# Scores of the second queries of batch 0 from 64-row tiles, and a hand-set order from the first instruction

## Chip, cores and metric

The kernel runs on one core of one Trainium2 chip. The metric is the device time of one execution in microseconds (us). The kernel before took 816.43 us, the median of three runs (814.87 to 817.64).

## The reference

Block-causal attention feeds a gated convolution network, all in float32:

```python
scores = q @ k.T / sqrt(64)                       # 8 batches, 8 heads, 576 tokens, 64 wide
scores = where(query block >= key block, scores, -1e9)       # blocks of 64 tokens
x = concat over heads of softmax(scores) @ v      # 8 x 576 x 512
h = relu(x @ w_in)                                # w_in 512 x 1024
gate = sigmoid(conv3(h, conv_w))                  # along tokens, one filter per column
out = (h * gate) @ w_out                          # w_out 1024 x 512
```

The three weights come as float64 and are decoded on the chip.

## The kernel before, in words

**Precision.** Matmuls take float32r operands. Each operand is held as a rounded part and a remainder (`qh`/`ql`, `kh`/`kl`, `wih`/`wil`), and a product is the sum of three matmuls: high by high, low by high, high by low.

**Visits.** The work is cut into visits, each for a pair of heads. Batch 0 gets four visits "A" (queries 0 to 255), then four visits "B" (queries 256 to 575). The other seven batches get 28 whole visits. During the A visits the weights `w_in` are loaded and decoded, during the B visits `w_out`. The feed-forward matmuls (`ffn`, L1142 and L1201) of a batch are spread over the visits that follow it.

**A visit.** Queries and keys are transposed on TensorE (`first_t` L741 for A, `stage_t` L671 for the others), and ScalarE and VectorE evict the high and low parts. For an A visit the two heads of a pair lie in partitions 0-63 and 64-127 of `qa`, `qb`, `kh`, `kl`, and `stage_sa` (L881) multiplies them there: matmuls of 64 rows, head 0 and head 1 by turns, into two PSUM banks (L894). For a B or whole visit, `stage_t` issues DMAs on SyncE's queue that build stacked operands of 128 rows: `qa`/`qb` (high over low of one head, L730), `ka`/`kb` (the high keys twice, L730), and `qz` (a head's high part with zeros in the other half, L708). `stage_s` (L765) then needs two matmuls of 128 rows per block of 128 queries and head: L815 (`ka`,`qa`) and L817 (`kl`,`qz`). In B visits a third one adds the mask (L811). Then come a maximum on VectorE (L825), exp with sums on ScalarE (L828), sum and reciprocal on VectorE (L779, L784) and a scaling on GpSimd (L790). The last 64 queries of both heads share a block of their own (L856). After that the probabilities are transposed (L975), split again (L985 to L994) and multiplied by the values (L1066).

**Order.** Every operation is an `Op` with a target time. `Plan.order` (L97) places all of them with a table of costs and writes out one fixed order for each engine. Where it expects TensorE to stand idle for more than `LEAST`, it inserts dummy matmuls (`work`, L1324, called fills here). They write a score bank that is about to be used, and do nothing else. Targets come from the constants at L264 to L303. Each engine works through its own list strictly in order. In the kernel before, `manual_schedule` is entered only for that list (L1329). What stands ahead of it (identities, mask tile, memsets of kept tiles, L331 to L365) is placed by the framework.

**Counters.** A DMA's end is signalled by one of eight counters, DMAHW0 to DMAHW7. They are dealt out by turns in the order in which the DMAs are recorded. A DMA that gets a counter which an earlier DMA holds is issued only after that one has landed. This wait stands in the queue of the engine that issues it.

**The start.** `load_first` (L431) loads queries, keys and values of batch 0 into `ptbh` and `ptbl`. The keys of pair 0 are issued from ScalarE's queue (L442), all else from SyncE's. The first real work is the transposes of pair 0 (L749).

Of the kernel before, what the change touches and what calls it, by code (L numbers as in the profile page):

```python
# [9 lines left out]
F32 = mybir.dt.float32  # L10
F32R = mybir.dt.float32r
# [222 lines left out]
def kernel(  # L234
# [29 lines left out]
    SLOT, SLOTA, SLOTB = 10.93, 3.2, 5.63  # L264
    WOFF, WSTEP, WLEAD = 1.32, 4.64, 8.03
    WOFF2, WSTEP2 = 38.12, 4.08
    OXA, OPVA, OTA = 3.27, 4.0, 0.13
    OXB, OPVB, OTB = 4.44, 11.35, 4.4
    OX, OPV, OT = 6.73, 18.46, 10.65
    VLEAD, NLEAD, NB, CONV = 2.32, 3.83, 7.53, -0.16  # L270
    OFA, OFB, OF, OXS = 3.54, 7.96, 1.07, 2.1
    FA, FB = 57.6, 86.67
# [3 lines left out]
    JS0, JS1, JS2, JS3, JS4, JS5, JS6, JS7 = -0.1, 0.0, 0.0, 0.0, 1.2, 0.0, 0.06, 0.0  # L276
    JX0, JX1, JX2, JX3, JX4, JX5, JX6, JX7 = 0.14, 0.64, 0.61, 0.25, 0.0, 0.0, 0.0, 1.14
    JP0, JP1, JP2, JP3, JP4, JP5, JP6, JP7 = 0.0, 0.51, 0.28, 1.31, 0.0, 0.67, -0.11, 0.07
    JT1, JT2, JT3, JT4, JT5, JT6, JT7, JT8 = 0.0, 0.0, 0.01, 0.2, -0.38, 0.64, 0.0, 0.0
    JW0, JW1, JW2, JW3, JW4, JW5, JW6, JW7 = 0.64, 2.05, -0.14, 0.0, 1.79, 0.0, 0.74, 1.76  # L280
    JW8, JW9, JWA, JWB, JWC, JWD, JWE, JWF = 0.12, 1.04, 0.06, -0.23, 0.0, -0.41, 0.0, 0.0
    JD0, JD1, JD2, JD3, JD4, JD5, JD6, JD7 = -2.82, 0.0, -1.25, 0.74, 2.2, -0.87, -1.36, 0.0
    JL8, JL9, JLA, JLB, JLC, JLD, JLE, JLF = 0.12, -0.07, 0.0, 0.0, -0.08, 0.0, -1.04, 0.41
# [5 lines left out]
    SKIP = 5.33  # L289
    LEAST, SPARE = 0.42, 0.11  # L290
# [6 lines left out]
    PMASK = ("B",)  # L297
# [3 lines left out]
    LQ, LQS, LV, LVS = -60.0, 7.42, -56.75, 4.18  # L301
    WL0, WLS = -55.92, 2.96
    WINDOW = 20.06  # L303
# [51 lines left out]

    ident = cp.tile([P, P], F32, tag="ident", name="ident")
# [195 lines left out]
    def split(f, parts, src, hi, lo, scratch, deps, bufs, at, go):  # L552
# [39 lines left out]
        o1 = pl.op(ACT, c_act(512), fh, at + 1, deps=[x[0] for x in o], bufs=bufs)  # L592
        o2 = pl.op(PE, c_mm(512), less, at + 1, deps=[o1], bufs=[fb])
        o2 = pl.op(PE, c_mm(512), rest, at + 1, deps=[o2] + [x[1] for x in o], bufs=bufs + [fb])
        wdone[f] = pl.op(DVE, c_dve(512, two_in=True) - 0.03, fl2, at + 1, deps=[o2], bufs=bufs + [fb])
# [168 lines left out]

    def stage_s(ops, hh, at, part, shared):  # L765
# [5 lines left out]
        st = keep([P, 16], F32, "st", 2, EPS)  # L771
        pb, done, exps = {}, {}, {}

        def finish(blocks, st, c0, t0):
            a, b_, w_ = c0 + blocks[0], c0 + blocks[-1] + 1, 2 if blocks[0] < 4 else 3

            def i1():
                x = 4 if blocks[0] == 4 else 4 + 2 * blocks[0]
                nc.vector.tensor_reduce(out=st.ap[:, a:b_],  # L779
                                        in_=st.ap[:, x:x + w_ * (b_ - a)].rearrange("p (n w) -> p n w", w=w_),  # L780
                                        op=ALU.add, axis=AX.X)

            def i2():
                nc.vector.reciprocal(st.ap[:, a:b_], st.ap[:, a:b_])  # L784

            o = pl.op(DVE, 0.15, i1, t0, deps=exps[4] if blocks[0] == 4 else [exps[x] for x in blocks], bufs=[st])
            o = pl.op(DVE, 0.12, i2, t0, deps=[o], bufs=[st])
            for x in blocks:
                def norm(pt=pb[x], col=c0 + x):
                    nc.gpsimd.tensor_scalar(out=pt.ap, in0=pt.ap, scalar1=st.ap[:, col:col + 1], scalar2=0.0,  # L790
                                            op0=ALU.mult, op1=ALU.add)

                w = 128 * (x + 1) if x < 4 else S
                if x in NORMS[part]:
                    def norm_a(pt=pb[x], col=c0 + x):
                        nc.scalar.activation(out=pt.ap, in_=pt.ap, func=AF.Copy, scale=st.ap[:, col:col + 1])

                    done[x] = pl.op(ACT, c_act(w, False, True), norm_a, t0 + 0.3, deps=[o], bufs=[st, pb[x]])
                    continue
                done[x] = pl.op(POOL, c_pool(w) + 0.08, norm, t0 + 0.3, deps=[o], bufs=[st, pb[x]])  # L800

        groups, pmask = GROUPS[part], part in PMASK
        for z, i in enumerate(i for g in groups for i in g):
# [33 lines left out]
            for g in groups:  # L837
                if g[-1] == i:
                    finish(g, st, 12, t0 + 1.2)
        if hh:  # L840
            return pb, done

        t0 = at + 1.3 * (4 if part is None else 2)
        st4 = keep([P, 16], F32, "st4", 2, EPS)
        p4 = one([P, S], F32, "p4")
        pb[4] = p4
        ms, es, banks = [], [], []
        for j in range(2):
            k0, k1 = HS * j, HS * j + HS
            sb = bank("s")  # L850
            banks.append(sb)

            def mm4(sb=sb, k0=k0, k1=k1):
                qdh, qdl = t["qz"].ap[:, S - 64:S + 64], t["qdl"].ap
                for n, (q_, k_) in enumerate(((qdh, "kh"), (qdl, "kh"), (qdh, "kl"))):
                    nc.tensor.matmul(sb.ap[:, 0:HS], q_, t[k_].ap[:, k0:k1], start=(n == 0), stop=(n == 2))  # L856

            def mx4(sb=sb, j=j):
                nc.vector.tensor_reduce(out=st4.ap[:, j:j + 1], in_=sb.ap[:, 0:HS], op=ALU.max, axis=AX.X)

            o = pl.op(PE, 3 * c_mm(HS), mm4, t0, deps=ready4, bufs=[sb, t["qz"], t["qdl"], t["kh"], t["kl"]])
            ms.append(pl.op(DVE, c_dve(HS), mx4, t0 + 0.3, deps=[o], bufs=[sb, st4]))

        def mm4b():
            nc.vector.tensor_reduce(out=st4.ap[:, 2:3], in_=st4.ap[:, 0:2], op=ALU.max, axis=AX.X, negate=True)

        o = pl.op(DVE, 0.07, mm4b, t0 + 0.3, deps=ms, bufs=[st4])
        for j in range(2):
            def ex4(j=j, sb=banks[j]):
                nc.scalar.activation(out=p4.ap[:, HS * j:HS * j + HS], in_=sb.ap[:, 0:HS], func=AF.Exp,  # L870
                                     bias=st4.ap[:, 2:3], accum_out=st4.ap[:, 4 + j:5 + j])

            es.append(pl.op(ACT, c_act(HS, True, True, True) + 0.04, ex4, t0 + 0.6, deps=[o], bufs=[banks[j], st4, p4]))

        exps[4] = es
        finish((4,), st4, 8, t0 + 1.2)
        return pb, done

    def stage_sa(ops, at):  # L881
        t, ready, _ = ops

        st = keep([P, 16], F32, "st", 2, EPS)
# [378 lines left out]
    def transposes(i, at):  # L1263
        p, part = visits[i]
        return first_t(first[0], first[1], p, at) if part == "A" else stage_t(nat[i], at, part)
# [12 lines left out]
    for i, (p, part) in enumerate(visits):  # L1278
# [8 lines left out]
        for hh in range(2):  # L1287
            n = 2 * i + hh
            b0 = base[n]
            js, jx, jp, jt = (JS[i], JX[i], JP[i], JT[i + 1]) if i < 8 else (0.0, 0.0, 0.0, 0.0)  # L1290
            if part != "A":
                sm = stage_s(ops, hh, b0 + js, part, None)
            elif hh == 0:
                both = stage_sa(ops, b0 + js)
            if part == "A":
# [33 lines left out]
    ctx.enter_context(tc.manual_schedule(engines=None))  # L1329
# [31 lines left out]
```

## Time and profile before

| | |
|---|---|
| median of three runs | 816.43 us |
| the profiled execution, whole | 816.58 us |
| its span, first to last instruction | 814.8 us |
| TensorE busy (matmul) | 798.7 us, 98% of the span |
| VectorE busy | 649.3 us, 80% |
| ScalarE busy | 622.4 us, 76% |
| GpSimd busy | 420.1 us, 52% |

The profiled execution has 1.8 us outside its span and is 0.15 us above the median. Line numbers are those of the kernel before. PE is TensorE, PEld its weight loads, DVE VectorE, ACT ScalarE, POOL GpSimd, SP SyncE; "SPq" and "ACTq" are the issues of DMAs on those engines' queues. Fills count as busy time of PE.

### The profile page before, as it was taken

How to read it: one execution, taken by the hardware profiler on the slowest of the kernel's cores; microseconds unless marked ns; L12 is line 12 of the kernel's file. 1: busy time of each engine (PE TensorE's matmuls, PEld its weight loads, DVE VectorE, ACT ScalarE, POOL GpSimd, SP SyncE). 2: the span in 40 equal slices, each digit the busy share in tenths (PEclk: the TensorE clock that was granted, in tenths of full speed). 3: DMA queues.
4: the chain of work that ended last, by engine and by line, in shares of the span. 5: the costliest groups of instructions: out<-in, count | busy, mean ns of one | idle time of the engine just before them, and what ended most of it. 6: DMA issues, size and time to landing. Idle time of an engine off the chain costs nothing.

```text
span 814.8 us, 17293 instructions
## 1 busy us (share of the span) xinstructions
PE 798.7 (98%) x5377; PEld 718.2 (88%) x5377; DVE 649.3 (80%) x1906; ACT 622.4 (76%) x1774; POOL 420.1 (52%) x591
## 2 busy tenths in 40 slices
PE   7999999999999999999999999999999999999998
PEld 5678889988999989899999989899999989899996
DVE  5979998988897868888897968888887968887541
ACT  4768888977887858788787958878787958877652
POOL 3344445666655645556455745555465645546331
PEclk9999999999999999999999999999999999999999
DMA  9437775555555545444555535445555435440001
GB/s 223 153 87 175 196 184 134 120 134 134 133 121 146 120 105 131 106 114 105 134 120 146 119 98 118 103 115 117 144 121 144 113 82 121 101 104 14 14 27 40
DMA packets 168256, 96.08 MB, mean 118 GB/s; under 512 B 136908, under 2 KB 142564, under 8 KB 168164
## 3 DMA queue, kind: packets, MB, share of 16 engines
q1 hardware_dynamic: 167620, 94.84, 48.8%
q8 instruction: 44, 0.72, 0.4%
q14 instruction: 48, 0.39, 0.2%
q10 hardware_dynamic: 544, 0.13, 0.1%
HBM read 38.82 MB, written 9.44 MB: 59 GB/s over the span
## 4 chain that ended last, share of the span: by engine, by line
PE 88%; DVE 5%; ACT 3%; SPq 1%; DMA 1%; issue 1%; POOL 1%; ACTq 0%; DVEq 0%
PE f L1142 22%; PE f L1201 21%; PE w L1066 11%; PE w L975 10%; PE s L815 5%; PE s L817 4%; PE w L1201 3%; PE w L691 3%; PE s L856 3%; PE s L1142 2%; PE s L1324 1%; DVE stage L523 1%; DVE st L825 1%; DMA vn<-in_v_dram 0%; SPq L730 0%
## 5 line engine op out<-in xcount | busy, mean ns | idle before, releaser
L790 POOL TENSOR_SCALAR p<-p,st 128x384 f32<-128x384 f32 (+4 forms) x272 | 150.7, 567 | 120.3 <-DVE st L784 80.7
L1182 POOL TENSOR_TENSOR gl<-t,gh 128x288 fp32r<-128x288 f32 (+2 forms) x128 | 103.2, 809 | 190.1 <-ACT gh L1179 127.0
L828 ACT ACTIVATE p<-s,st 128x128 f32<-128x128 f32 (+1 forms) x240 | 128.6, 536 | 44.4 <-DVE st L825 41.9
L975 PE MATMUL w<-ident,p 128*128 128x128 f32 (+1 forms) x800 | 123.4, 275 | 0.3 <-DVE s L822 0.2
L825 DVE TENSOR_REDUCE st<-s 128x1 f32<-128x128 f32 (+1 forms) x240 | 117.4, 491 | 5.2 <-PE s L811 2.1
L985 ACT ACTIVATE ptbh<-w 128x384 fp32r<-128x384 f32 (+2 forms) x192 | 92.2, 507 | 26.2 <-PE w L975 25.4
L975 PEld LDWEIGHTS w<-ident,p 128*128 128x128 f32 (+1 forms) x800 | 93.4, 140 | 14.8 <-issue 3.8
L1201 PE MATMUL f<-woh,gh 128*128 128x512 f32 x248 | 105.2, 424 | 0.1
L988 DVE TENSOR_TENSOR ptbl<-w,ptbh 128x512 fp32r<-128x512 f32 (+1 forms) x144 | 87.9, 635 | 13.3 <-ACT ptbh L985 12.4
L1201 PE MATMUL f<-woh,gl 128*128 128x512 f32 x248 | 98.1, 396 | 0.0
L1201 PE MATMUL f<-wol,gh 128*128 128x512 f32 x248 | 98.0, 395 | 0.0
L1142 PE MATMUL f<-xh,wil 128*128 128x290 f32 (+2 forms) x480 | 96.8, 304 | 0.0
L1142 PE MATMUL f<-xh,wih 128*128 128x290 f32 (+2 forms) x480 | 94.3, 304 | 0.0
L1142 PE MATMUL f<-xl,wih 128*128 128x290 f32 (+2 forms) x480 | 93.7, 303 | 0.0
L1163 DVE SCALAR_TENSOR_TENSOR t<-f,cw,t 128x287 f32<-128x287 f32 (+3 forms) x120 | 59.7, 498 | 24.7 <-ACT t L1159 24.2
L817 PE MATMUL s<-kl,qz 128*128 128x128 f32 (+1 forms) x240 | 78.0, 325 | 0.0
L1142 PEld LDWEIGHTS f<-xh,wih 128*128 128x128 f32 x480 | 74.1, 190 | 1.4
L1142 PEld LDWEIGHTS f<-xh,wil 128*128 128x128 f32 x480 | 74.0, 188 | 1.0
L1142 PEld LDWEIGHTS f<-xl,wih 128*128 128x128 f32 x480 | 73.4, 189 | 0.6
L1159 ACT ACTIVATE t<-f,cw 128x288 f32<-128x288 f32 (+2 forms) x120 | 59.9, 499 | 5.8 <-ACT f L1156 0.4
L1179 ACT ACTIVATE gh<-t 128x288 fp32r<-128x288 f32 (+2 forms) x128 | 56.8, 445 | 9.1 <-DVE t L1175 8.5
L1167 DVE SCALAR_TENSOR_TENSOR t<-f,cw,t 128x288 f32<-128x288 f32 (+3 forms) x120 | 60.1, 501 | 1.0
(178 smaller groups left out, 1978.9 us busy)
## 6 DMA issues: line engine op xcount, KB each, us to landing
kn<-in_k_dram SPq DMA_DIRECT2D x64, 144.0 KB, 3.0
ka<-kh SPq DMA_DIRECT2D x64, 144.0 KB, 2.8
kb<-kh SPq DMA_DIRECT2D x64, 144.0 KB, 2.7
out_dram<-stage SPq DMA_DIRECT2D x36, 256.0 KB, 2.1
vn<-in_v_dram SPq DMA_DIRECT2D x64, 128.0 KB, 2.6
qn<-in_q_dram SPq DMA_DIRECT2D x56, 144.0 KB, 3.1
qa<-qh SPq DMA_DIRECT2D x28, 144.0 KB, 3.2
qb<-qh SPq DMA_DIRECT2D x28, 144.0 KB, 3.2
```

The costliest lines, as they stand in the source:

```text
L790: nc.gpsimd.tensor_scalar(out=pt.ap, in0=pt.ap, scalar1=st.ap[:, col:col + 1], scalar2=0.0, op0=ALU.mult, op1=ALU.add)
L817: nc.tensor.matmul(sb.ap[:, 0:nk], qz.ap[:, z:z + 128], kl.ap[:, 0:nk], start=False, stop=True)
L825: nc.vector.tensor_reduce(out=st.ap[:, i:i + 1], in_=sb.ap[:, 0:nk], op=ALU.max, axis=AX.X, negate=True)
L828: nc.scalar.activation(out=pt.ap[:, 0:nk], in_=sb.ap[:, 0:nk], func=AF.Exp, bias=st.ap[:, i:i + 1], accum_out=st.ap[:, 4 + 2 * i:5 + 2 * i])
L975: nc.tensor.matmul(tb.ap[0:kk, col:col + P], pb[x].ap[:, 128 * c:128 * c + kk], ident, start=(z == 0), stop=True, is_transpose=True, skip_ ...
L985: nc.scalar.activation(out=hi(), in_=src(), func=AF.Copy)
L988: nc.vector.tensor_tensor(out=lo(), in0=src(), in1=hi(), op=ALU.subtract)
L1066: nc.tensor.matmul(tb.ap[0:m, q0 - qa:qb - qa], vv.ap[:, chunk(c), hh, w[ps_]], pm.ap[:, 128 * c + q0:128 * c + qb] if qa == 0 else pm.ap[ ...
L1142: nc.tensor.matmul(fb.ap[:, 0:n2], wt[:, c, fs], xs[c][xi].ap[:, x0:x0 + n2], start=(n + c - c0 == 0), stop=(n + c - c0 == 3 * NCC - 1))
L1167: nc.vector.scalar_tensor_tensor(out=t.ap[:, 0:i1], in0=fb.ap[:, own + 1:own + 1 + i1], scalar=cw[:, 2 * NFC + f:2 * NFC + f + 1], in1=t.a ...
L1182: nc.gpsimd.tensor_tensor(out=gbuf[1].ap[:, f, carry:carry + no], in0=t.ap[:, 0:no], in1=gbuf[0].ap[:, f, carry:carry + no], op=ALU.subtract)
L1201: nc.tensor.matmul(fb.ap[:, 0:DM], gbuf[a].ap[:, f, cs], w[:, f, :], start=(f == 0 and n == 0), stop=(f == NFC - 1 and n == 2))
```

## The change

For the B visits `rest_t` takes the place of `stage_t`. It leaves the two heads in the two halves of the partitions, and moves only four pieces of 64x64 by DMA, for the block of the last 64 queries. `stage_sb` takes the place of `stage_s`: three matmuls of 64 rows per block and head, head 0 and head 1 by turns, both heads at once in the two "s" banks, and a mask matmul of 64 rows each. Sums and reciprocals of both heads are taken together. `finish` and `last_s` are the old code, moved out of `stage_s`. The tile `st` gets four buffers instead of two. The zeroing of `qz` and `qdl` goes from VectorE to GpSimd. `manual_schedule` is entered ahead of the first instruction. Nearly all constants of the order are set anew. The options `WPA` and `FHP` are added but empty.

```diff
-    SLOT, SLOTA, SLOTB = 10.93, 3.2, 5.63
+    SLOT, SLOTA, SLOTB = 10.98, 3.2, 6.01
...
-    PMASK = ("B",)
+    PMASK = ()
+    BBANK = (("s", "s"), ("s", "s"))
...
-                nc.vector.memset(t.bitcast(F32), value)
+                (nc.gpsimd if tag[0] == "q" else nc.vector).memset(t.bitcast(F32), value)
...
+    ctx.enter_context(tc.manual_schedule(engines=None))
     ident = cp.tile([P, P], F32, tag="ident", name="ident")
...
-    nc.scalar.activation(out=maskt[0:64, :], in_=ident[0:64, 0:64], func=AF.Copy, scale=0.0, bias=MASKED)
-    nc.scalar.activation(out=maskt[64:P, :], in_=ident[64:P, 0:64], func=AF.Copy)
+    nc.scalar.activation(out=maskt, in_=ident[:, 0:64], func=AF.Copy, scale=0.0, bias=MASKED)
...
+    def rest_t(nat, at):
+        t = {nm: two([P, S], F32R, nm) for nm in ("kh", "kl", "qa", "qb")}
...
+            if which == 0:
+                for src, dst, c_ in ((hi, t["qz"], S - 64), (lo, t["qdl"], 0)):
+                    for o_ in (0, 64):
+                        def mv4(o_=o_, src=src, dst=dst, c_=c_):
+                            nc.sync.dma_start(out=dst.ap[o_:o_ + 64, c_ + o_:c_ + o_ + 64].bitcast(F32),
+                                              in_=src.ap[o_:o_ + 64, S - 64:S].bitcast(F32))
...
+    def stage_sb(ops, at):
...
+        for z, i in enumerate((2, 3)):
+            nk = 128 * (i + 1)
+            sb = [bank(x) for x in BBANK[z]]
...
+                for n, (q_, k_) in enumerate((("qa", "kh"), ("qb", "kh"), ("qa", "kl"))):
+                    for hh in range(2):
+                        r = slice(64 * hh, 64 * hh + 64)
+                        nc.tensor.matmul(sb[hh].ap[:, 0:nk], t[q_].ap[r, qs], t[k_].ap[r, 0:nk], start=(n == 0), stop=(n == 2))
+                for hh in range(2):
+                    r = slice(64 * hh, 64 * hh + 64)
+                    nc.tensor.matmul(sb[hh].ap[0:64, nk - 64:nk], rident[r, r], maskt[r, :], start=False, stop=True,
+                                     skip_group_check=True)
...
-    ctx.enter_context(tc.manual_schedule(engines=None))
     for o in pl.order(WINDOW, SKIP, (work, NBANK, 0.234, LEAST, SPARE), CLOCK):
```

**The start of ScalarE's queue.** `ptbh<-in_k_dram` are the two halves of the keys of pair 0, `kh` and `qa` the evictions of the first transposes. Before:

```order
L443 DMA ptbh<-in_k_dram 128x2x64 x2
L361 ACT_TABLE_LOAD
L361 ACTIVATE nident<-ident 128x128 [waits Pool_49]
L364 ACTIVATE maskt<-ident 64x64
L365 ACTIVATE maskt<-ident 64x64
L753 ACTIVATE kh<-w 128x256 [waits PE_49]
L753 ACTIVATE qa<-w 128x256 [waits PE_49]
```

And in the changed kernel, on the same queue:

```order
L366 ACT_TABLE_LOAD
L366 ACTIVATE nident<-ident 128x128 [waits Pool_49]
L368 ACTIVATE maskt<-ident 128x64
L446 DMA ptbh<-in_k_dram 128x2x64 [waits DMAHW3_49]
L446 DMA ptbh<-in_k_dram 128x2x64 [waits DMAHW5_49]
L773 ACTIVATE kh<-w 128x256 [waits PE_49]
L773 ACTIVATE qa<-w 128x256 [waits PE_49]
```

The two loads of the keys went from the first place behind the table load and the mask tile, and each now has a counter that a DMA of SyncE's queue held first.

That queue, SyncE's, starts like this in the kernel before (`ptbl<-in_v_dram` are values, `gh<-in_moe_w_in_dram` is a slice of `w_in`):

```order
L443 DMA ptbh<-in_q_dram 128x2x64 x2
L606 DMA gh<-in_moe_w_in_dram 128x4x256
L454 DMA ptbl<-in_v_dram 128x4x64 x2
L606 DMA gh<-in_moe_w_in_dram 128x4x256
L443 DMA ptbh<-in_q_dram 128x2x64 [waits DMAHW0_49]
L443 DMA ptbh<-in_q_dram 128x2x64 [waits DMAHW1_49]
```

And in the changed kernel:

```order
L446 DMA ptbh<-in_q_dram 128x2x64 x2
L457 DMA ptbl<-in_v_dram 128x4x64 x2
L626 DMA gh<-in_moe_w_in_dram 128x4x256
L446 DMA ptbh<-in_q_dram 128x2x64 x2
L446 DMA ptbh<-in_k_dram 128x2x64
L446 DMA ptbh<-in_k_dram 128x2x64 [waits DMAHW0_49]
```

The values moved ahead of the weights. Dealt out by turns, counters 0 and 1 go to the queries of pair 0, 2 and 3 to the values, 4 to the weights, and 5 and 6 to the queries of pair 1. So DMAHW3 is held by the second half of the values and DMAHW5 by the first half of pair 1's queries.

**TensorE, the first B visit.** Names: `s` a score bank, `w` and `f` other banks. Before, around the scores of its first head:

```order
L584 MATMUL f<-woh,nident 128x512
L587 MATMUL f<-wol,rident 128x512
L1324 MATMUL s<-rident 128x512
L815 MATMUL s<-ka,qa 128x384
L817 MATMUL s<-kl,qz_101 128x384
L811 MATMUL s<-maskt,rident 128x64
L815 MATMUL s<-ka,qa 128x512
L817 MATMUL s<-kl,qz_101 128x512
L811 MATMUL s<-maskt,rident 128x64
```

And in the changed kernel, from the mask of its first block (384 keys, both heads) to the second block (512 keys):

```order
L963 MATMUL s<-maskt,rident 64x64 x2
L1115 MATMUL w<-ptah,nident 128x384
L1190 MATMUL w<-ptah,vv 64x256
L1190 MATMUL w<-ptah,vv 64x128 x2
L1190 MATMUL w<-ptah,vv 64x256
L801 MATMUL w<-ident,qn 128x80 x4
L587 MATMUL f<-wih,nident 128x512
L1190 MATMUL w<-ptal,vv 64x128
L1190 MATMUL w<-ptal,vv 64x256
L1266 MATMUL f<-xh,wih 128x256 x2
L1450 MATMUL w<-rident 128x512 x2
L960 MATMUL s<-kh,qa 128x512 x2
```

Before, the two blocks of a head stood back to back, each in a bank of its own. Now a block takes both score banks, one for each head, and ten rows of other work stand between a block and the next one in the same two banks. Over the whole program, fills go from 104 to 102, and SyncE's DMAs from 749 to 713.

More of the change, by code (lines that the diff above doesn't have):

```diff
@@ L769, in stage_s @@
         qz = t["qz"]
-        st = keep([P, 16], F32, "st", 2, EPS)
+        st = keep([P, 16], F32, "st", 4, EPS)
         pb, done, exps = {}, {}, {}
[L774 to L800, printed above, removed]
         groups, pmask = GROUPS[part], part in PMASK
@@ L838, in stage_s @@
                 if g[-1] == i:
-                    finish(g, st, 12, t0 + 1.2)
+                    finish(g, st, 12, t0 + 1.2, pb, done, exps, part)
         if hh:
             return pb, done
[L843 to L873, printed above, removed]
@@ L881, in stage_sa @@
     def stage_sa(ops, at):
         t, ready, _ = ops
-        st = keep([P, 16], F32, "st", 2, EPS)
+        st = keep([P, 16], F32, "st", 4, EPS)
         sb = [bank("s"), bank("f")]
@@ L1264, in transposes @@
         p, part = visits[i]
-        return first_t(first[0], first[1], p, at) if part == "A" else stage_t(nat[i], at, part)
+        if part == "A":
+            return first_t(first[0], first[1], p, at)
+        return rest_t(nat[i], at) if part == "B" else stage_t(nat[i], at)
     def values(i, at):
@@ L1290 @@
             js, jx, jp, jt = (JS[i], JX[i], JP[i], JT[i + 1]) if i < 8 else (0.0, 0.0, 0.0, 0.0)
[L1291 to L1295, printed above, removed]
+            if not part:
+                sm = stage_s(ops, hh, b0, part, None)
+            else:
+                if hh == 0:
+                    both = (stage_sa if part == "A" else stage_sb)(ops, b0 + js)
                 sm = both[hh]
```

173 lines of the change are left out of this document (150 added, 23 removed).

## The prediction

> **What bounds the kernel now.** I read the page first, then busy time by stage, then what TensorE waited for, then the first microseconds in order of time.
>
> ```profile
> span 814.8 us, 17293 instructions
> PE 798.7 (98%) x5377; PEld 718.2 (88%) x5377; DVE 649.3 (80%) x1906; ACT 622.4 (76%) x1774; POOL 420.1 (52%) x591
> L1324 PE MATMUL s<-rident 128*128 128x512 f32 x98 | 31.1, 433 | 3.8 <-DVE rident L359 3.8
> ```
>
> TensorE is busy for 98% of the span. Its 31.1 us of fills are the other kind of waste. A change can shorten the run by less real work on TensorE, fewer fills, less idle time, or less time at a low clock. The stages tell where there is any:
>
> ```profile
> 0.00:10.00 10.00, 6.16 (x27) 4.70 (x27) 3.44 (x11) 3.42 (x7) 1.38 (x8) 1.00 0.85 207
> 10.00:50.00 40.00, 37.69 (x215) 25.97 (x211) 33.78 (x91) 26.71 (x80) 17.91 (x34) 1.00 0.58 144
> 50.00:90.00 40.00, 37.98 (x276) 33.45 (x275) 34.37 (x102) 32.84 (x91) 16.86 (x24) 1.00 0.72 171
> 90.00:120.00 30.00, 27.03 (x179) 23.64 (x177) 28.51 (x81) 24.61 (x70) 14.62 (x19) 0.94 0.80 192
> 120.00:200.00 80.00, 79.33 (x551) 71.74 (x550) 71.98 (x224) 66.33 (x195) 45.77 (x65) 1.00 0.59 137
> 200.00:780.00 580.00, 579.46 (x3973) 531.54 (x3972) 466.09 (x1377) 453.36 (x1298) 317.11 (x438) 1.00 0.46 110
> ```
>
> Columns: stretch, length, busy PE, PEld, DVE, ACT, POOL, granted clock. From 200 to 780 us PE idles 0.54 us in all, so the whole visits have nothing to gain. Idle time is 3.84 us at the start, 2.31 in the A visits (10 to 50), 2.02 and 2.97 in the B visits (50 to 120). From 90 to 120 DVE is 95% busy (28.51 of 30) and the clock is 0.94. So everything the change can win lies in the first 120 us. What PE waited for in the whole span:
>
> ```profile
> PE s L1324 <- DVE rident L359: 3.8, 1, 3.8
> PE s L815 <- DMA ka<-kh: 1.9, 2, 0.9
> PE f L584 <- ACT woh L568: 1.6, 2, 0.9
> PE f L584 <- ACT wih L568: 0.8, 4, 0.2
> ```
>
> The second row is the moved keys: two waits, 1.9 us, the only ones that a moved operand of a B visit causes.
>
> **Part 1, the scores on TensorE.** One head's two blocks in a B visit before:
>
> ```profile
> 84.99 0.34 PE L815 MATMUL s<-ka,qa 128*128 128x384 f32 x1
> ...
> 85.34 0.20 PE L811 MATMUL s<-maskt,rident 128*128 128x64 f32 x1
> 85.38 0.47 PE L815 MATMUL s<-ka,qa 128*128 128x512 f32 x1
> ...
> 85.96 0.41 PE L991 MATMUL w<-ptbh,nident 128*128 128x384 f32 x1
> ```
>
> Start to start this takes 0.97 us, and 7.8 us for eight heads. The 64-row form already runs in the A visits:
>
> ```profile
> 27.47 0.33 PE L894 MATMUL s<-kh,qa 64*128 64x256 f32 x1
> 27.47 0.33 PE L894 MATMUL f<-kh,qa 64*128 64x256 f32 x1
> 27.64 0.28 PE L894 MATMUL s<-kh,qb 64*128 64x256 f32 x1
> ...
> 27.76 0.27 PE L894 MATMUL s<-kl,qa 64*128 64x256 f32 x1
> ...
> 28.00 0.44 PE L991 MATMUL w<-ptah,nident 128*128 128x384 f32 x1
> ```
>
> Both heads start at once, so a pair costs one matmul. The step from pair to pair is 0.17 (the first) and 0.12 us for 256 columns, 0.47 ns a column, and the step out to a 128-row matmul is 0.24, which is 0.12 more than the pair's own. So three pairs, the extra 0.05, the exit 0.12 and the mask 0.04 (as L811 above) make 0.75 us for 384 keys and 0.93 for 512, 1.68 a visit, 6.7 for four. That saves 1.1 us if the way in is free, and 0.3 if it costs 0.1 for each of the eight blocks (no row isolates it). I take 0.6. The Trainium skill, page TensorEngine Tiling (Array Packing), section Key Properties, says that a change of tiling mode drains TensorE; the exit of 0.24 agrees. By the section Theoretical Speedup of that page of the Trainium skill (up to 2x at 64 rows), with no drain, the saving would be about 2.4 us, an estimate from that page.
>
> Without the pairing the change would add 5.0 us: 3 x (0.18 + 0.24) us more a visit, four times. The equal starts speak against that.
>
> **Part 2, moves and small operations.** The moves of keys and queries go, and with them the 1.9 us of waits on `ka`. What comes next is the eviction of `kl` and `qb`, one step earlier in the same chain, and it lies under the same feed-forward work, so I keep the whole 1.9 (bounds 1.0 and 1.9). SP's 36 fewer DMAs cost PE nothing elsewhere. Fills fall from 104 to 102; a warm one is 4.13/17 = 0.24 us (the fence of part 3), so 0.5 us. On DVE, two sums and two reciprocals go per visit:
>
> ```profile
> L784 DVE RECIPROCAL st<-st 128x1 f32<-128x1 f32 x20 | 3.1, 154 | 0.1
> L779 DVE TENSOR_REDUCE st<-st 128x1 f32<-128x2 f32 (+1 forms) x20 | 2.9, 147 | 0.7 <-POOL p L790 0.3 <-ACT p L828 0.2
> ```
>
> This is 2 x 0.154 + 2 x 0.147 = 0.6 us a visit, 2.4 in all. It shortens the run only where DVE holds PE, from 90 to 120, about two visits: at most 1.2 us, and I take 0.6. The clock of 0.94 over 30 us costs 1.8 us there. No other stage has a lower clock, and none has so many waits, so I take half back, 0.9 (bounds 0 and 1.8). Sum of parts 1 and 2: 0.6 + 1.9 + 0.5 + 0.6 + 0.9 = 4.5 us gained.
>
> **Part 3, the start.** The static order moves the first loads of keys. The first microseconds before:
>
> ```profile
> 0.73 1.02 ACTq L443 DMA_DIRECT2D ptbh<-in_k_dram  x2
> 0.73 0.96 SPq L443 DMA_DIRECT2D ptbh<-in_q_dram  x2
> 2.25 1.06 SPq L454 DMA_DIRECT2D ptbl<-in_v_dram  x2
> 3.35 0.51 SPq L606 DMA_DIRECT2D gh<-in_moe_w_in_dram  x1
> 3.84 2.07 PE L1324 MATMUL s<-rident 128*128 128x512 f32 x4 [3.84 <-DVE rident L359]
> 5.71 0.63 PE L749 MATMUL w<-ident,ptbh 128*128 128x128 f32 x2
> ...
> 7.70 1.55 PE L1324 MATMUL s<-rident 128*128 128x512 f32 x4
> 9.18 0.32 PE L894 MATMUL s<-kh,qa 64*128 64x128 f32 x1
> 10.06 4.13 PE L1324 MATMUL s<-rident 128*128 128x512 f32 x17
> ```
>
> and how long loads took from issue to landing (last column), the keys and queries first, then the values, then pair 1's first query load:
>
> ```profile
> ptbh<-in_k_dram ACTq DMA_DIRECT2D x1, 64.0 KB, 2.5
> ptbh<-in_q_dram SPq DMA_DIRECT2D x1, 64.0 KB, 2.3
> ...
> ptbh<-in_k_dram ACTq DMA_DIRECT2D x1, 64.0 KB, 3.2
> ...
> ptbl<-in_v_dram SPq DMA_DIRECT2D x1, 128.0 KB, 4.5
> ...
> ptbh<-in_q_dram SPq DMA_DIRECT2D x1, 64.0 KB, 5.3
> ```
>
> Before, both halves of the keys were issued at 0.73 and had landed when PE came to them at 5.71 us. In the changed order the first half waits for the second half of the values, SP's fourth DMA. SP's issues follow every 0.5 us (the fourth and fifth before start at 2.25, the sixth at 3.35), so it goes out at about 2.25 and lands 2.3 to 4.5 later; only 256 KB are ahead of it and no weights, so I take 2.6, which is 4.85. The second half waits for pair 1's first query load, SP's sixth DMA: issued at 3.35, landing 2.3 to 5.3 us later. Before, it had a megabyte of weights ahead of it, now half of that; I take 3.4, which is 6.75. The keys then need 2.5 to 3.2 us themselves: 2.85, so the second half is there at 9.6 us. Its transpose was PE's second of two, at 5.71 + 0.21 = 5.92. That is 3.7 us late. PE has then stood for six microseconds, so the fills behind it run like the first four (2.07 us for four, against 1.48 from 7.70 to 9.18): 0.4 more. **The first scores come 4.1 us later than before** (bounds: 2.1, if every load takes its shortest time, and 6.5, if each takes its longest).
>
> Does anything absorb it? ACT, DVE and PE all have the eviction or transpose of pair 0 as their first real work, and stand in order behind it, fills included. From 10 to 50 us PE's waits were on ACT and DVE, none on a load. So the whole program shifts, and I let all of it count. That `rident` is ready about 2 us earlier (no memsets ahead of it on DVE) gains nothing, since PE then waits for the keys. The zeroing on POOL lies under that wait too. The Trainium skill, page DMA: Bandwidth & Descriptors, section Anatomy of one DMA, says that DMA engines do not wait on semaphores: the wait is on the issuing sequencer, before dispatch. By that rule the keys' whole transfer starts after the counter; were it hidden, the sum would be 4.1 us less. No row here shows such a wait on ACT's queue.
>
> **Sum.** 816.58 - 4.5 + 4.1 = 816.2 us against the profiled execution, which lies 0.15 above the median: 816.0 us. A measurement of this kernel tells 0.3%, 2.4 us, from no change.
>
> **Rivals.** *The B visits give more (faster).* DVE, relieved, no longer holds PE from 90 to 120: the 2.97 us of idle time and the 1.8 us of clock all go, with 0.6 + 1.9 + 0.5 from above 7.8, and the start costs 3.0: 811.8 - 0.15, about 811.7. For it speaks that DVE is at 95% only there. Against it: 1.6 us of PE's waits are on decoded `w_out` (the row of `woh`), whose decoding the change leaves as it is.
>
> *The score banks turn round too slowly (slower).* A block now takes both banks, so the next needs both heads' maximum and exp first:
>
> ```profile
> L828 ACT ACTIVATE p<-s,st 128x384 f32<-128x384 f32 (+3 forms) x19 | 11.6, 610 | 2.7 <-DVE st L825 2.4 <-POOL p L790 0.2
> L825 DVE TENSOR_REDUCE st<-s 128x1 f32<-128x384 f32 x9 | 4.9, 549 | 2.2 <-PE s L811 2.1
> ```
>
> Two maxima and the second head's exp are 0.55 + 0.55 + 0.61 = 1.7 us, near 2 with the way between engines. The ten rows between the blocks of the first visit have 3,904 columns, about 1.8 us of PE at 0.47 ns a column. If each of eight blocks waits 0.5 us, that is 4 us: 820.0. It decides from where DVE or ACT comes to a block late by more than the cover. *The pairs do not overlap (the change doesn't do what it says):* 5.0 us more, 821.0.
>
> **How the numbers follow.** Forecast 0.42 (no change that can be measured), more from the B visits 0.35, banks 0.20, no overlap 0.03. So faster 0.35, same 0.42, slower 0.23. The range takes in the first rival at its 811.7 and the second at 820.0: 811.5 to 820.2. The forecast's own range, from the bounds 2.1 and 6.5 of the start, is 814 to 818.4.
>
> **What would show it.** Right: the key loads on ACT's queue issue at about 5 and 7 us, first scores at about 13.3 us, no wait on `ka` in B visits, B blocks whose pairs start together 0.18 and 0.24 us apart, and less than 5 us idle from 50 to 120 after a start with some 7 us idle. Wrong: first scores before 11 us, or PE idle from 90 to 120 under 0.5 us (faster); waits of L960 on exp, or of `last_s` on the banks (slower); or PE idle from 200 on, which I put at no change.

## The result, and the profile after

The changed kernel takes 823.02 us (median, 820.97 to 823.61) where the kernel before, with a fourth run beside the three above, takes 816.19 (814.87 to 817.64): a ratio of 1.0079, interval 1.0054 to 1.0104. It is slower, and the forecast of 816.0 with its range of 811.5 to 820.2 was wrong. The profiled execution took 823.61 us, with a span of 821.8, 7.0 more than before. Line numbers from here on are those of each kernel's own code.

The page of the changed kernel, its head and the engines' busy time, and the group of fills from the lines kept apart by shape:

```profile
span 821.8 us, 17261 instructions
...
PE 798.0 (97%) x5391; PEld 716.0 (87%) x5391; DVE 648.0 (79%) x1888; ACT 619.6 (75%) x1773; POOL 422.7 (51%) x595
...
L1450 PE MATMUL s<-rident 128*128 128x512 f32 x96 | 30.0, 431 | 3.7 <-DVE st L335 3.7
```

Span less busy PE is PE's idle time: 821.8 - 798.0 = 23.8 us, against 814.8 - 798.7 = 16.1 before. So TensorE is busy 0.7 us less and stands 7.7 us longer. The whole loss is idle time. By stage (columns as in the prediction: busy PE, PEld, DVE, ACT, POOL, granted clock, DMA share, GB/s):

```profile
0.00:10.00 10.00, 2.52 (x5) 1.34 (x5) 2.34 (x7) 1.74 (x3) 5.17 (x14) 1.00 0.72 193
10.00:50.00 40.00, 34.47 (x189) 25.03 (x191) 27.22 (x75) 22.69 (x65) 12.51 (x23) 1.00 0.55 143
50.00:90.00 40.00, 39.03 (x290) 31.96 (x289) 36.35 (x102) 34.45 (x99) 19.18 (x28) 1.00 0.34 88
90.00:120.00 30.00, 28.12 (x198) 23.50 (x197) 26.51 (x72) 25.20 (x69) 15.43 (x20) 0.94 0.49 130
120.00:200.00 80.00, 77.41 (x538) 69.92 (x536) 68.87 (x215) 66.36 (x194) 44.20 (x62) 1.00 0.58 140
200.00:780.00 580.00, 578.37 (x3978) 531.43 (x3977) 475.15 (x1395) 452.80 (x1308) 316.55 (x439) 1.00 0.46 111
```

Idle time rises by 3.6 us up to 10 us (7.48 against 3.84) and by 3.2 from 10 to 50 (5.53 against 2.31). From 50 to 120 it falls by 2.1 (2.85 against 4.99), as the change was forecast to bring. From 120 to 200 it rises again by 1.9 (2.59 against 0.67), and from 200 to 780 by 1.1. The first scores come 7.82 us later than before (below), so a fixed stretch doesn't hold the same work in both kernels. These are the start, the A visits and the B visits (50 to 120 before) of the changed kernel, moved by that much:

```profile
0.00:17.82 17.82, 6.90 (x27) 4.68 (x27) 3.19 (x9) 3.07 (x6) 5.78 (x15) 1.00 0.87 217
17.82:57.82 40.00, 37.10 (x214) 26.60 (x211) 32.63 (x91) 26.56 (x79) 15.38 (x28) 1.00 0.35 97
57.82:127.82 70.00, 67.95 (x489) 57.12 (x488) 63.03 (x175) 60.62 (x168) 33.62 (x45) 0.98 0.48 125
```

Idle time is then 10.92 at the start (3.84 before), 2.90 in the A visits (2.31), 2.05 in the B visits (4.99), and 2.59 and 1.63 behind them as in the fixed stretches (0.67 and 0.54). So there are two losses, 7.1 us at the start and 3.0 after the B visits, and a gain of 2.9 in the B visits. TensorE's longest waits of the whole span name the first loss:

```profile
PE w L769 <- DMA ptbh<-in_k_dram: 7.2, 2, 3.7
PE s L1450 <- DVE st L335: 3.7, 1, 3.7
PE f L587 <- DVE st L878: 1.7, 1, 1.7
PE f L587 <- ACT wih L571: 1.4, 4, 0.4
PE s L914 <- ACT t L1296: 1.4, 1, 1.4
```

The first row, the transposes of pair 0's keys, is new. The 1.9 us on `ka` in the B visits are gone. The first microseconds in order of time:

```profile
1.25 2.05 POOL L335 MEMSET qz<- 128x1152 f32 x2
1.34 2.33 DVE L364 TENSOR_SCALAR rident<-ident 128x128 fp32r<-128x128 f32 x1 [1.34 <-POOL ident masks.py:199]
1.73 1.01 SPq L457 DMA_DIRECT2D ptbl<-in_v_dram  x2
...
3.34 1.02 SPq L446 DMA_DIRECT2D ptbh<-in_q_dram  x2
...
3.73 2.07 PE L1450 MATMUL s<-rident 128*128 128x512 f32 x4 [3.73 <-DVE st L335]
...
5.34 3.28 ACTq L446 DMA_DIRECT2D ptbh<-in_k_dram  x2
...
9.50 0.45 PE L769 MATMUL w<-ident,ptbh 128*128 128x128 f32 x1 [3.70 <-DMA ptbh<-in_k_dram]
...
13.44 0.47 PE L769 MATMUL w<-ident,ptbh 128*128 128x128 f32 x1 [3.50 <-DMA ptbh<-in_k_dram]
...
17.00 0.32 PE L1018 MATMUL s<-kh,qa 64*128 64x128 f32 x1
```

and from issue to landing, pair 1's first query load (issued at 3.34), then the first and the second key load:

```profile
ptbh<-in_q_dram SPq DMA_DIRECT2D x1, 64.0 KB, 4.9
...
ptbh<-in_k_dram ACTq DMA_DIRECT2D x1, 64.0 KB, 4.0
...
ptbh<-in_k_dram ACTq DMA_DIRECT2D x1, 64.0 KB, 5.1
```

The keys' first half goes out at 5.34, behind the values' second half, and lands at 5.34 + 4.0 = 9.34. The second ends its issue at 5.34 + 3.28 = 8.62; it goes out near 8.2, behind pair 1's first query load (landed at 3.34 + 4.9), and lands near 13.3. TensorE takes each at once (9.50 and 13.44). The first scores come at 17.00 us instead of 9.18: 7.8 us late, where 4.1 was forecast with 6.5 as the outer bound.

The B visits themselves went as written. A block of 384 keys for both heads:

```profile
85.12 0.45 PE L960 MATMUL s<-kh,qa 64*128 64x384 f32 x2
85.40 0.35 PE L960 MATMUL s<-kh,qb 64*128 64x384 f32 x2
85.57 0.35 PE L960 MATMUL s<-kl,qa 64*128 64x384 f32 x2
85.75 0.20 PE L963 MATMUL s<-maskt,rident 64*64 64x64 f32 x2
85.89 0.67 PE L1115 MATMUL w<-ptbh,nident 128*128 128x384 f32 x2
```

Each row is two matmuls, one for each head. The third row starts 0.17 us behind the second and the mask 0.18 behind the third, the time of one matmul of 384 columns at the prediction's 0.47 ns a column, so the heads overlap. Start to start a block takes 0.77 us (0.75 forecast); the block of 512 keys, from 92.40 to 93.32, takes 0.92 (0.93 forecast).

### The profile page after: what moved, and what is told of

It is laid out like the page before. It is cut to its first block, busy times and chain, and to the rows that moved or that the text cites. A ratio compares the mean times of both kernels' runs of the same rounds, so it can differ in the third digit from the quotient of the medians.

```text
span 821.8 us, 17261 instructions
## 1 busy us (share of the span) xinstructions
PE 798.0 (97%) x5391; PEld 716.0 (87%) x5391; DVE 648.0 (79%) x1888; ACT 619.6 (75%) x1773; POOL 422.7 (51%) x595
## 4 chain that ended last, share of the span: by engine, by line
PE 78%; ACT 9%; DVE 7%; DMA 2%; issue 2%; SPq 1%; POOL 0%; ACTq 0%; DVEq 0%
PE f L1325 20%; PE f L1266 18%; PE w L1190 9%; PE w L1099 8%; PE s L914 4%; PE s L916 4%; PE w L1325 3%; PE s L869 3%; PE w L711 3%; PE s L1266 2%; ACT p L927 1%; ACT ptbh L1109 1%; DVE t L1287 1%; ACT p L1040 1%; PE s L960 1%
## 5 line engine op out<-in xcount | busy, mean ns | idle before, releaser
L843 POOL TENSOR_SCALAR p<-p,st 128x256 f32<-128x256 f32 (+4 forms) x256 | 140.9, 565 | 171.6 <-DVE st L837 113.7
L927 ACT ACTIVATE p<-s,st 128x128 f32<-128x128 f32 x224 | 118.5, 530 | 41.4 <-DVE st L924 39.3
L924 DVE TENSOR_REDUCE st<-s 128x1 f32<-128x128 f32 x224 | 107.6, 485 | 3.7
L1099 PEld LDWEIGHTS w<-ident,p 128*128 128x128 f32 (+1 forms) x800 | 95.9, 140 | 14.3 <-POOL p L1055 2.3
L1109 ACT ACTIVATE ptbh<-w 128x384 fp32r<-128x384 f32 (+1 forms) x192 | 92.8, 504 | 15.5 <-PE w L1099 14.9
L1112 DVE TENSOR_TENSOR ptbl<-w,ptbh 128x512 fp32r<-128x512 f32 (+1 forms) x144 | 89.8, 633 | 11.9 <-ACT ptbh L1109 8.8
L1266 PE MATMUL f<-xh,wih 128*128 128x290 f32 (+2 forms) x480 | 97.0, 305 | 0.0
L916 PE MATMUL s<-kl,qz 128*128 128x128 f32 x224 | 72.1, 322 | 0.0
L1296 ACT ACTIVATE t<-t 128x288 f32<-128x288 f32 (+2 forms) x128 | 56.6, 443 | 13.3 <-DVE t L1291 12.4
```

Of the source, the lines that this page charges most:

```text
L916: nc.tensor.matmul(sb.ap[:, 0:nk], qz.ap[:, z:z + 128], kl.ap[:, 0:nk], start=False, stop=True)
L924: nc.vector.tensor_reduce(out=st.ap[:, i:i + 1], in_=sb.ap[:, 0:nk], op=ALU.max, axis=AX.X, negate=True)
L927: nc.scalar.activation(out=pt.ap[:, 0:nk], in_=sb.ap[:, 0:nk], func=AF.Exp, bias=st.ap[:, i:i + 1], accum_out=st.ap[:, 4 + 2 * i:5 + 2 * i])
L1099: nc.tensor.matmul(tb.ap[0:kk, col:col + P], pb[x].ap[:, 128 * c:128 * c + kk], ident, start=(z == 0), stop=True, is_transpose=True, skip_ ...
L1109: nc.scalar.activation(out=hi(), in_=src(), func=AF.Copy)
L1112: nc.vector.tensor_tensor(out=lo(), in0=src(), in1=hi(), op=ALU.subtract)
```

## The experiments

**The theory and its rivals.** Theory: the late keys cost everything, the whole delay of the first scores passes to the end, and the rest of the change gains about what was forecast. First rival: the start is hidden, and the new B visits are slower than the old (turn-round of the banks). Second rival: the new constants alone are the loss. All runs are timed against the kernel before on the same chip, in two groups: its median was 816.66 us beside the first four kernels and 816.93 beside the other four.

**Keys first.** The changed kernel with pair 0's two key loads recorded ahead of everything else, so that they take the first counters and stand first on ScalarE's queue; the order of all other work stays. The counters of the other first loads are dealt out anew by that.

```diff
+    qk0 = cp.tile([P, 2, 2, H, D], F32, tag="ptbh", name="ptbh")
+    for c in range(2):
+        nc.scalar.dma_start(out=qk0[:, 1, c, 0:2, :], in_=k[0, 0:2, 128 * c:128 * c + 128, :].rearrange("h p d -> p h d"))
     ident = cp.tile([P, P], F32, tag="ident", name="ident")
...
+        qk.t = qk0
...
+                        if z and p0 == 0:
+                            return
```

> The changed kernel, but the two loads of pair 0's keys are recorded ahead of all else, so they are issued first on ScalarE's queue and wait for no counter; the order of all compute work stays. Theory 'start' (the late keys cost what they delay the first scores, and everything behind them shifts): first scores at about 9.5 us instead of 17.0, and the whole 7.5 us comes back: about 815.5 us, ratio to before 0.999. Rival 'absorbed' (the B visits catch up part of any late start, and the loss lies in the later order of the whole visits): at most 4 us come back, 819 us or more, ratio 1.003 or more, with PE still idle some 4 us from 120 to 780 us.

Measured: 813.36 us (813.0 to 815.0), ratio 0.9965, interval 0.9953 to 0.9977. With only the two loads moved, the change is 0.35% faster than the kernel before. The first scores came at 9.56 as expected; about 2 us more than the expected 7.5 came back, which is taken up below. Its timeline, at the start and at the two blocks shown above:

```profile
0.73 1.02 ACTq L363 DMA_DIRECT2D ptbh<-in_k_dram  x2
...
9.56 0.34 PE L1024 MATMUL s<-kh,qa 64*128 64x128 f32 x1
...
77.67 0.44 PE L966 MATMUL s<-kh,qa 64*128 64x384 f32 x2
...
84.94 0.50 PE L966 MATMUL s<-kh,qa 64*128 64x512 f32 x2
```

Against the changed kernel the first scores differ by 17.00 - 9.56 = 7.44 us, the two blocks by 85.12 - 77.67 = 7.45 and 92.40 - 84.94 = 7.46. Over 75 us of program nothing absorbs any of the delay. That decides against the first rival: the B visits' work is unchanged here, and the loss is gone. Its stages from 50 us on show where the gain is, and where some is given back:

```profile
50.00:120.00 70.00, 67.89 (x498) 57.33 (x499) 63.42 (x177) 61.36 (x171) 33.94 (x45) 1.00 0.50 126
120.00:200.00 80.00, 77.85 (x542) 70.51 (x542) 70.06 (x222) 66.10 (x193) 47.17 (x67) 1.00 0.54 133
200.00:780.00 580.00, 578.97 (x3970) 531.91 (x3969) 467.89 (x1369) 448.15 (x1294) 313.75 (x434) 1.00 0.45 110
```

From 50 to 120 PE idles 2.1 us instead of 4.99; from 120 to 200 it idles 2.15 instead of 0.67, and from 200 to 780 1.03 instead of 0.54.

**The old kernel with the early static order.** The kernel before, with `manual_schedule` entered ahead of the first instruction and nothing else changed. That also puts `rident` ahead of the memsets on VectorE.

```diff
+    ctx.enter_context(tc.manual_schedule(engines=None))
     ident = cp.tile([P, P], F32, tag="ident", name="ident")
...
-    ctx.enter_context(tc.manual_schedule(engines=None))
     for o in pl.order(WINDOW, SKIP, (work, NBANK, 0.234, LEAST, SPARE), CLOCK):
```

> The kernel before with one edit: the hand-set order is entered ahead of the first instruction, as in the changed kernel. Its key loads then wait for the counters of the second half of the values and of pair 1's first query load, with a slice of weights ahead of them. Theory 'start': first scores 8 us or more late, time 823 to 826 us, ratio 1.009 to 1.012. Rival 'absorbed': at most 820 us, ratio 1.004.

Measured: 824.88 us (824.29 to 826.18), ratio 1.0108, interval 1.0093 to 1.0123. Its start and its longest wait:

```profile
7.30 2.25 ACTq L444 DMA_DIRECT2D ptbh<-in_k_dram  x2
...
17.04 0.47 PE L895 MATMUL s<-kh,qa 64*128 64x128 f32 x1
```

```profile
PE w L750 <- DMA ptbh<-in_k_dram: 9.1, 2, 7.6
```

This came as expected. One line brings the same late first scores, 17.04 - 9.18 = 7.86 us later, and costs 824.88 - 816.66 = 8.2 us (7.7 between the two profiled spans). Here the keys are issued at 7.30, as the two loads take their counters behind other DMAs. The delay passes to the end one for one in the old order of the work, too.

**The new scores alone, and the new constants alone.** The first kernel has the changed code with the constants of before, the late static order and the zeroing on VectorE. The second has the code of before with the new constants. Both start with early keys. A line or two of some twenty in each edit:

```diff
 # the new scores alone (against the changed kernel)
-    SLOT, SLOTA, SLOTB = 10.98, 3.2, 6.01
+    SLOT, SLOTA, SLOTB = 10.93, 3.2, 5.63
...
-                (nc.gpsimd if tag[0] == "q" else nc.vector).memset(t.bitcast(F32), value)
+                nc.vector.memset(t.bitcast(F32), value)
...
 # the new constants alone (against the kernel before)
-    SLOT, SLOTA, SLOTB = 10.93, 3.2, 5.63
+    SLOT, SLOTA, SLOTB = 10.98, 3.2, 6.01
```

> The 64-row scores of the B visits alone: the changed kernel's code with the constants of the kernel before, its late entry of the hand-set order, and the zeroing on VectorE. Theory 'start' with the forecast gain of the B visits: 812 to 815 us, ratio 0.995 to 0.999, no wait on moved keys in B visits. Rival 'banks' (both score banks for one block make the next block wait): 818 us or more, ratio above 1.002, with waits ahead of the scores of B visits.

> The new constants alone in the kernel before (mask still added in its B visits, start and operands as before). Theory 'start': the constants are worth little: 815 to 818 us, ratio 0.998 to 1.002. Rival 'constants' (the new targets of the whole visits cost the 3 us of idle time that PE shows from 120 to 780 us after the change): 819 us or more, ratio above 1.003, with that idle time.

Measured: the scores alone 816.95 us (815.87 to 817.68), ratio 1.0004, interval 0.9996 to 1.0013; the constants alone 820.61 (818.49 to 821.55), ratio 1.0047, interval 1.0034 to 1.0060. Both expectations of the theory were missed (812 to 815, and 815 to 818). The first gains nothing. The waits of TensorE with the scores alone, where `wol` is the low half of decoded `w_out`:

```profile
PE f L589 <- DVE wol L536: 1.7, 2, 1.0
...
PE f L1324 <- DVE wol L592: 0.8, 1, 0.8
```

The waits on `ka` are gone, and waits on the decoding of `w_out` have taken their place: 1.7 and 0.8 us. With the new constants on the old scores there are again two waits on `ka`, but the longer one stands in a whole visit, and the stages after 120 us idle more:

```profile
PE s L815 <- DMA ka<-kh: 1.8, 2, 1.2
```

```profile
157.95 0.30 PE L815 MATMUL s<-ka,qa 128*128 128x128 f32 x1 [1.20 <-DMA ka<-kh]
```

```profile
120.00:200.00 80.00, 77.83 (x539) 70.26 (x540) 69.59 (x222) 66.95 (x197) 46.00 (x64) 1.00 0.59 137
200.00:780.00 580.00, 578.02 (x3965) 531.12 (x3964) 472.18 (x1383) 450.43 (x1301) 315.86 (x438) 1.00 0.47 110
```

In the B visits 0.6 of the 1.9 us on `ka` is left. From 120 to 780 us PE idles 2.17 + 1.98 = 4.15 us instead of 1.21, which is what the rival 'constants' said, with its time of 819 us or more. The fixed order also writes more fills into both kernels, 114 with the scores alone and 111 with the constants alone, against 104 before and 102 in the changed kernel. So neither part pays by itself.

**Both, with the late static order.** The changed kernel with `manual_schedule` back where it stood; the zeroing stays on GpSimd.

```diff
-    ctx.enter_context(tc.manual_schedule(engines=None))
     ident = cp.tile([P, P], F32, tag="ident", name="ident")
...
+    ctx.enter_context(tc.manual_schedule(engines=None))
     for o in pl.order(WINDOW, SKIP, (work, NBANK, 0.234, LEAST, SPARE), CLOCK):
```

> The changed kernel with its hand-set order entered late, as in the kernel before; scores, constants and GpSimd's zeroing as changed. It is the fourth cell beside the kernel before, b_only and table_only. Theory 'start': the same as keys_first, since the keys go out first again: 812.5 to 814.5 us, ratio 0.995 to 0.998. Rival: the early entry did some good of its own apart from the keys: 815 us or more.

Measured: 813.87 us (812.62 to 814.37), ratio 0.9962, interval 0.9950 to 0.9975, as expected; first scores at 8.33. With a healthy start the four corners are 816.9 (neither), 816.95 (scores), 820.6 (constants) and 813.9 (both): the two gain 3.1 us together and nothing apart. The corner with both also has the zeroing on GpSimd, which the corner with the scores alone has not; their first scores are 0.28 us apart (8.33 and 8.61). The second rival falls as the cause of the loss, since a kernel with the new constants and early keys is faster. But the idle time that it named is there: from 120 to 780 us PE idles 3.0 to 4.6 us in all seven traces with the new constants (3.8 in this one), and 1.2 to 2.2 in the three without them.

**Half of the keys late.** As keys first, but the second half is issued behind the mask tile and gets a counter of the values' second half.

```diff
-    for c in range(2):
+    for c in range(1):
         nc.scalar.dma_start(out=qk0[:, 1, c, 0:2, :], in_=k[0, 0:2, 128 * c:128 * c + 128, :].rearrange("h p d -> p h d"))
...
-                        if z and p0 == 0:
+                        if z and p0 == 0 and c == 0:
                             return
```

> As keys_first, but only the first half of pair 0's keys goes first; the second half stands behind the mask tile and waits for the counter of the second half of the values. It is a smaller dose of the same delay. Theory 'start': that load goes out at 5.3 us and lands at about 9.3, first scores at about 13 us instead of 9.56, and all of it shows: about 817 us. Rival 'absorbed' (a small delay is hidden): at most 815 us.

Measured: 819.14 us (815.67 to 820.09), ratio 1.0018, interval 1.0005 to 1.0031. Its timeline:

```profile
5.02 0.40 ACTq L452 DMA_DIRECT2D ptbh<-in_k_dram  x1
...
9.59 0.48 PE L775 MATMUL w<-ident,ptbh 128*128 128x128 f32 x1 [3.87 <-DMA ptbh<-in_k_dram]
...
13.04 0.32 PE L1024 MATMUL s<-kh,qa 64*128 64x128 f32 x1
```

The load and the first scores came as expected, the time 2 us above the expected 817. The first scores are 3.48 us later than with keys first. Each against its own kernel before, this one loses 2.2 us and keys first gains 3.3, so the time is 5.5 us longer: a middle dose gives a middle loss. Its runs spread over 4.4 us, and by the two intervals the loss is 2.3 to 6.4 us, so the 2.0 above the delay are not clear of the noise. This start is also the one that the forecast assumed (first scores at 13.3). Even so the kernel is 2.2 us slower than before, where the forecast had it 0.4 faster: the gain was overrated too.

**Keys first, zeroing on VectorE.** The zeroing of `qz` and `qdl` goes back to VectorE, where the early static order leaves it behind `rident`; the rest is the kernel with keys first.

```diff
-                (nc.gpsimd if tag[0] == "q" else nc.vector).memset(t.bitcast(F32), value)
+                nc.vector.memset(t.bitcast(F32), value)
```

> As keys_first, and the zeroing of qz and qdl is back on VectorE, behind rident. Theory 'port' (VectorE's rident took 2.33 us instead of 0.2 because GpSimd's zeroing ran beside it, and PE's first fills waited for it): rident takes 0.2 us, the first fills start at 1.6 us instead of 3.7, the keys' landing at about 4.5 us is then the bound, first scores at about 8.3 us instead of 9.56, and the time falls by the same 1.2 us: about 812.1 us. Rival: the zeroing costs nothing on the path, 813.4 us.

Measured: 812.02 us (811.14 to 813.66), ratio 0.9942, interval 0.9929 to 0.9956. It is the best version, ahead of both kernels. Its start:

```profile
1.33 0.23 DVE L367 TENSOR_SCALAR rident<-ident 128x128 fp32r<-128x128 f32 x1 [1.33 <-POOL ident masks.py:199]
...
1.62 2.07 PE L1456 MATMUL s<-rident 128*128 128x512 f32 x4 [1.62 <-DVE rident L367]
...
7.29 0.32 PE L1024 MATMUL s<-kh,qa 64*128 64x128 f32 x1
```

`rident` takes 0.23 us here and 2.33 in the changed kernel, where GpSimd zeroes beside it. The first scores come at 7.29, a microsecond earlier than expected: the keys' landing was not the bound. That is 2.27 us earlier than with keys first, and the time falls by 1.6, from 3.3 to 4.9 us below the kernel before of its group. Most of the rest shows as idle time from 10 to 50 us, 3.49 instead of 2.83. So the expected time was met with two steps of it wrong.

**Keys on SyncE's queue.** Another remedy, in the changed kernel: all keys and queries go out on SyncE's queue, keys first in its order, and the zeroing is on VectorE.

```diff
-                        eng = nc.scalar if src is k and p0 == 0 else nc.sync
+                        eng = nc.sync
```

> The changed kernel, but the keys of pair 0 are issued from SyncE's queue, where they stand first and wait for no counter; the zeroing is on VectorE behind rident. Theory 'start': keys landed by 3.6 us and queries by 4.6, first scores at about 8.3 us, about 812 us; the 1 us by which all other loads go out later costs nothing. Rival: the later weights delay the decoding, 813.5 us or more.

Measured: 813.70 us (812.39 to 814.54), ratio 0.9962, interval 0.9949 to 0.9974; first scores at 7.34. It is the landing of the keys that counts, not the engine that issues them. At the same first scores it stands 1.7 us behind the version before it, and above the 813.5 of the rival. But the intervals of the two overlap, their profiled spans are 811.5 here and 811.9 there, and PE idles less from 10 to 50 us here (3.14 against 3.49), so later decoding doesn't show.

## Why the prediction was wrong, point by point

**Two steps failed: the size of the start, and the stages after 120 us, which stood at nothing.** The forecast was 7.0 us too low, 816.0 against 823.02. With 7.8 us for the start its sum gives 819.7, so the start is about half of that; the rest is the gain, which is taken up behind it. The start: "The first scores come 4.1 us later than before (bounds: 2.1, if every load takes its shortest time, and 6.5, if each takes its longest)." (Its own terms add up to 6.3 as the longest and to 2.2, or 2.6 with the slow fills, as the shortest; the difference changes nothing.) The mechanism was right, down to the two counters and the order of issue, and so was the sentence after it, that the whole program shifts. Measured are 7.8 us, of which the sum lacks 3.7. It splits into the two landings that the second half hangs on. Pair 1's first query load took 4.9 us, where 3.4 was taken, and released its counter at about 8.2 us instead of 6.75, which is 1.5. The key load then took 5.1 us instead of 2.85, which is 2.25. The 2.85 was the mean of 2.5 and 3.2, rows of loads that went out at 0.73 us, ahead of all weights. In the new order the keys go out at 5.34 and 8.2, when weights and values are on their way from SyncE's queue. Rows for such a place stood in the prediction: 4.5 us for the values and 5.3 for pair 1's queries. (The values' second half, taken at 2.6, took about 3.1: out at 2.24, its counter free at 5.34.) The upper bound failed for the same reason: it took 3.2 as the longest time of a key load. With the two measured times, 4.9 and 5.1, the same working gives the 17 us. That traffic is why the loads are slow is argued from these rows; no run took the traffic away.

By the Trainium skill, page DMA: Bandwidth & Descriptors, section Anatomy of one DMA, the wait stands on the issuing sequencer, before dispatch (the section is on DMAs of GpSimd, the sentence on DMA engines at large). The key loads' issues at 5.34 and about 8.2, each after its counter came free, agree.

**The gain of 4.5 us** was too large, and its terms came out differently. The changed kernel loses 6.8 us with first scores 7.8 late, which leaves a gain of 1.0. With the start repaired the gain is 3.1 (late static order, first scores 0.85 earlier than before) to 3.3 (keys first, 0.38 later). If the start is paid one for one, the rest gains 1.4 to 3.7 us in the four repaired kernels (keys on SyncE's queue the least, keys first the most), and 1.7 with half of the keys late. In the kernel with keys first:

- Idle time from 50 to 120 fell by 2.9 us. The forecast had 2.5, of waits on `ka` and of DVE's small operations. But the scores alone show that this part does not all come with the removal of the waits (1.4 of the 2.9); without new constants, decoding takes over. I had put it down to the change of the scores.
- Idle time after 120 us grew by 1.5 + 0.5 = 2.0 us, and in the changed kernel by 1.9 + 1.1 = 3.0. This is the second step that failed. The prediction read from the little idle time there "the whole visits have nothing to gain", and put nothing down for what they could lose, though the change sets nearly all constants of their order anew. The constants alone show it: 2.9 us more in the old kernel. In the changed kernel its longest piece is the 1.4 us on L1296 in the fence of waits above.
- PE is busy 3.0 us less than before (795.7 against 798.7), and that is most of the gain that is left. In the changed kernel it is 0.7. The fills into the score banks cost 30.0 us there instead of 31.1, a little more than the 0.5 forecast. A visit's two blocks took 0.77 + 0.92 = 1.69 against the 1.68 that gave the 0.6.
- The clock, 0.9 forecast, is no gain of the change. From 90 to 105 us the profile of before has 0.89, the changed kernel 0.90, keys first 1.00, and keys first with zeroing on VectorE, the fastest, 0.89 again. The kernel before shows both itself: of its runs beside the experiments, 12 with a mean clock of 1.000 average 816.55 us, and 15 at 0.998 or less 817.00, which is hardly more than their scatter.

**The delay at the end looks larger than at the start.** The profiled spans of the changed kernel and of keys first differ by 821.8 - 811.2 = 10.6 us, not 7.44; the medians by some 9.7. Matching the same matmuls of the two traces shows where it arises: the delay is 7.4 to 7.5 us up to 92 us, 9.0 from 100 on, 10.2 at 240 and 10.5 at 780. The first step, 1.5 us, is the clock. These are 3.41 us of the changed kernel, and of keys first with the zeroing on VectorE and on GpSimd, the last two in the same place of the work:

```profile
101.96:105.37 3.41, 3.41 (x19) 2.79 (x17) 0.79 (x4) 2.64 (x7) 2.34 (x4) 0.50 0.73 206
```

```profile
92.24:95.65 3.41, 3.33 (x17) 2.88 (x16) 1.76 (x6) 2.64 (x9) 2.06 (x3) 0.50 0.65 187
```

```profile
93.54:96.95 3.41, 3.33 (x28) 2.75 (x27) 2.16 (x7) 3.41 (x11) 2.79 (x4) 1.00 0.66 190
```

At a clock of 0.50 PE gets through 17 matmuls in the time of 28. The profile of keys first happens to be without that stretch. Against the version with the zeroing on VectorE, which has it, the spans differ by 821.8 - 811.9 = 9.9 us, and the first scores by 17.00 - 7.29 = 9.71. The later steps, 0.3 to 0.7 us each, differ from version to version; their cause stays open. In the runs' times no excess is clear of the noise: by the intervals the changed kernel stands 6.3 to 12.3 us behind keys first, and 7.4 lies inside. So the loss of 6.8 us is the 7.8 of the start less 1.0, in which the idle time after 120 us eats most of the gain in the B visits and in busy time.

**`rident`** was to be ready about 2 us earlier. It wasn't: its operation ran 2.33 us beside GpSimd's zeroing, and the first fills began at 3.73 instead of 3.84. I had this at no gain, and in the changed kernel it has none, since the keys come later still. With early keys the zeroing no longer lies under their wait: there it sets the first fills, and taking it off GpSimd brings the 1.6 us.

**The rivals.** *Banks:* not borne out. No matmul of L960 waits as long as 0.5 us in the changed kernel, the mark that I set, and with early keys the same banks run in a faster kernel. The time that this rival gave, 820.0, was nearer to the measured one than mine, and that is chance. *The B visits give more:* the idle time there did fall, by 2.9 of 4.99 us, but two thirds of that returns after 120 us, and from 90 to 120 PE still idles 1.9. *No overlap:* its 821.0 was the nearest of all, and it is refuted by the pairs, which step by 0.17 us where it needed twice that.

## What to carry to other kernels

Time a transfer that moves later in the program by rows of transfers issued at its new place in the traffic, not by its own row at the old one: here 4.0 to 5.1 us instead of 2.5 to 3.2. Price the stages that a new order touches for what they can lose too, even where there is nothing to gain: here 2 to 3 us. When an order becomes static, look first at which semaphore each of the first loads waits on, since a load can hang on another queue's transfer that has nothing to do with its data. And try constants that were tuned for a change together with it: here one alone gained nothing, the other lost 4 us, and both gained 3.

## What the runs showed of the hardware that was not expected

A VectorE operation on 128x128 numbers took 2.33 us while GpSimd zeroed two tiles beside it, and 0.23 us with the zeroing on VectorE itself; with the late static order, where it began at 2.30 us, it took 1.33. The same 64 KB load landed 2.5 to 3.2 us after an issue at 0.73, and 4.0 to 5.1 us after one at 5 to 8 us. Seven of the ten profiles have one stretch of 3.41 us at a granted clock of 0.50 between 92 and 106 us, behind waits of PE of 0.7 to 1.7 us; keys first, with the same 1.7 us wait, has none.
